# Block sums for a seven-product second layer: vector additions, or scalar copies with accumulating transfers

## The chip, the core and the metric

The kernel runs on one core of one Trainium2 chip. A core has a matrix engine (PE, with its weight loads PEld), a vector engine (DVE), a scalar engine (ACT), GpSimd (POOL) and a sync engine (SP); each takes its own instructions in order, and engines wait for each other and for transfers through semaphores. ACT, SP and POOL also issue DMAs, and the instruction that issues one stands in line with the engine's other work. The metric is the device time of one execution in microseconds (us), lower is better. Two runs of the kernel before took 622.52 and 622.56 us, a median of 622.54.

## The reference

A gated linear recurrence in float32, followed by a two-layer network with a leaky gate:

```
B, H, S, D = 4, 8, 768, 48
f = 1 / (1 + exp(-f_logit))
for t in range(S):
    state = f[:, :, t, :, None] * state + k[:, :, t] outer v[:, :, t]
    y[:, :, t] = q[:, :, t] @ state
x = y.transpose(0, 2, 1, 3).reshape(3072, 384)
h = x @ w_in                                   # 384 x 2048
g = maximum(h, 0) + alpha * minimum(h, 0)
out = g @ w_out                                # 2048 x 384
```

## The kernel before

The tokens are cut into twelve steps. A step is a pair of batches and a chunk of C = 128 positions: T = 256 tokens, in two halves `u` (one batch each). Every step goes through four generators: `prepare` (key P: loads, sigmoid, products of decays, on DVE and ACT), `carry` (O: the state), `attend` (S: the attention matrix `A`, the result `py` and its transposed copy `xT`) and `network` (n: both layers). A string written out by hand (`FIRST`, `USUAL`, lines 31 to 37) says in which order the pieces between two `yield`s are issued. PE, DVE and ACT keep exactly this order. While pass m of the network runs, `attend` of step m+1 and `prepare` of step m+2 are woven into it: "USUAL" is `S n2 S n2 O2 n Q n3 Q n Q S3 n Q S n Q n Q n`, where Q is a piece of the next `prepare`. POOL and SP are not in the manual order; a scheduler places what they issue.

The first layer runs in eight pieces `f` (L613). Each makes two blocks of 128 hidden rows in one PSUM bank `ph` (L618, twelve matmuls as the program writes them, shown in the trace as passes of 128x256), ACT writes `neg` = relu(-h) (L623, two buffers), and DVE writes the two blocks of `gate` (L625). Pass 0 multiplies `gate` by `w_out` plainly. Passes 1 to 11 split `gate` into token halves u and hidden halves j, split `w_out` into four blocks, and use seven products instead of eight (L657, 8 matmuls of the program, 16 in the trace, 2.60 us each product). For this they need four sums of gate blocks, S (one tile, one buffer), made by `sums` (L693) after f = 3 for the first four f and after f = 7 for the rest, and fixed differences of `w_out` blocks, made once (`halves_of_w_out`, L704). With a11 = (u0, j0), a12 = (u0, j1), a21 = (u1, j0), a22 = (u1, j1):

```
s1 = a21 + a22    s2 = s1 - a11    s3 = a11 - a21    s4 = a12 - s2
```

The five pieces behind f = 7 issue, on PE: `pa`, `pb`; then, after the pieces of `attend` between them (ACT copies `ad` into `A`, L563; PE multiplies `py`, L574), `pc`, `pd`; then `pa` and `pc` once more, added in place; then `pe`. DVE adds the products up (`plus`, L661; `kept`, `u2`, `u3` in `late["C"]`, called Csum in the profile). Four PSUM banks (`psn`) serve `ph` and all products, so a new one waits until the one before it in its bank has been read.

Between the pieces on ACT stand the copies of `qd` into `us` for the next step (L314), `kept` (L668), the eight copies into `A` (L563), the copies of `py` into `y` (L583) and the DMAs `xT<-y` (L603, dealt to SP, ACT and POOL). POOL issues the loads of q, f, k (L266) and v (L276). SP issues 16 small DMAs a step, `ksn<-kt` (L427), and the stores.

Of the kernel before, what the change touches and what calls it, by code (L numbers as in the profile page):

```python
# [8 lines left out]
F32 = mybir.dt.float32  # L9
# [5 lines left out]
AF = mybir.ActivationFunctionType  # L15
ALU = mybir.AluOpType

C = 128
# [3 lines left out]
U = 2  # L22
# [6 lines left out]
UP = 2.0 ** 16  # L29
# [29 lines left out]
def kernel(  # L59
# [30 lines left out]
    nc = tc.nc  # L90
    B, NC, _, HP, _ = qT.shape
    DM = v.shape[-1]
# [5 lines left out]
    T = U * C  # L98
# [16 lines left out]
    const = ctx.enter_context(tc.tile_pool(name="const", bufs=1))  # L115
# [9 lines left out]
    def bank(name):  # L125
        return psn.tile([128, 512], F32, tag="net", name=name)

    om = const.tile([128, NF], F32, tag="om", name="om")
    w_in_sb = const.tile([128, NK, DF], F32, tag="w_in", name="w_in_sb")
    w_out_sb = const.tile([128, NF, DM], F32, tag="w_out", name="w_out_sb")  # L130
    NH, DH = NF // 2, DM // 2
    gate = const.tile([128, NH, 2, T], F32, tag="gate", name="gate")
    lvl = const.tile([128, 2, DB], F32, tag="lvl", name="lvl")
    nc.scalar.dma_start(out=lvl, in_=masks)
    nc.scalar.dma_start(out=om, in_=alpha)
# [27 lines left out]
    for m in range(1, NB):  # L163
        lo = UO[m] + (4 if m == 1 else 0)
        n = NB - m
# [4 lines left out]
    for half in range(2):  # L170
        for m in range(1, NQ):
            n = NQ - m
# [436 lines left out]
    def network(bp, c, x):  # L609
        i = f"{bp}_{c}"  # L610
        xT = x["T"]
        plain = (bp, c) == steps[0]
        for f in range(NH):  # L613
            ph = bank(f"ph{f}_{i}")
            tiles = (2 * f, 2 * f + 1) if plain else (f, f + NH)
            for kt in range(NK):
                for j, m in enumerate(tiles):
                    nc.tensor.matmul(ph[:, j * T:(j + 1) * T], lhsT=w_in_sb[:, kt, m * 128:(m + 1) * 128],  # L618
                                     rhs=xT[:, kt], start=(kt == 0 and j == 0), stop=(kt == NK - 1 and j == 1),
                                     skip_group_check=True)  # L620
            neg = work.tile([128, 2, T], F32, tag="neg", name=f"neg{f}_{i}")
            phv = ph.rearrange("p (j t) -> p j t", j=2)
            nc.scalar.activation(neg, phv, AF.Relu, scale=-1.0)  # L623
            for j, m in enumerate(tiles):
                nc.vector.scalar_tensor_tensor(gate[:, m % NH, m // NH], neg[:, j], om[:, m:m + 1], phv[:, j],  # L625
                                               ALU.mult, ALU.add)
            if not plain and f % 4 == 3:
                sums(slice(f - 3, f + 1))
            yield

        def store(u, o):
            t0 = ((U * bp + u) * NC + c) * C
            nc.sync.dma_start(out=out[t0:t0 + C], in_=o)

        if plain:
            po = [bank(f"po{u}_{i}") for u in range(U)]
            for n, (f, u) in enumerate([(f, u) for f in range(NF) for u in range(U)]):
                nc.tensor.matmul(po[u][:, 0:DM], lhsT=gate[:, f % NH, f // NH, u * C:(u + 1) * C], rhs=w_out_sb[:, f],  # L638
                                 start=(f == 0), stop=(f == NF - 1))
                if n % 8 == 7 and n != U * NF - 1:  # L640
                    yield
            for u in range(U):
                o = work.tile([128, DM], F32, tag="o", name=f"o{u}_{i}")
                nc.scalar.activation(o, po[u][:, 0:DM], AF.Copy, scale=UP)
                store(u, o)
            yield
            return

        a11, a12, a22 = (lambda f, j=j, u=u: gate[:, f, j, u * C:(u + 1) * C] for j, u in ((0, 0), (1, 0), (1, 1)))
        s1, s2, s3, s4 = (lambda f, n=n: late["S"][:, n, f] for n in range(4))  # L650
        b11, t1, b21, b22 = (lambda f, r=r, d=d: w_out_sb[:, NH * r + f, DH * d:DH * (d + 1)]
                             for r, d in ((0, 0), (0, 1), (1, 0), (1, 1)))
        t2, t3, t4 = (lambda f, t=t: late[t][:, f] for t in ("t2", "t3", "t4"))

        def product(to, of, by, more=False):
            for f in range(NH):
                nc.tensor.matmul(to[:, 0:DH], lhsT=of(f), rhs=by(f), start=(f == 0 and not more), stop=(f == NH - 1),  # L657
                                 skip_group_check=True)

        def plus(to, of, by, scale=UP):  # L660
            nc.vector.scalar_tensor_tensor(to, of[:, 0:DH], scale, by, ALU.mult, ALU.add)  # L661

        o0, o1 = (work.tile([128, DM], F32, tag="o", name=f"o{u}_{i}") for u in range(U))
        kept, u2, u3 = (late["C"][:, n] for n in range(3))
        pa, pb = (bank(f"p{n}_{i}") for n in "ab")
        product(pa, a11, b11)
        product(pb, a22, t4)
        nc.scalar.activation(kept, pa[:, 0:DH], AF.Copy, scale=UP)  # L668
        yield
        pc, pd = (bank(f"p{n}_{i}") for n in "cd")  # L670
        product(pc, s2, t2)
        product(pd, s1, t1)
        plus(u2, pc, kept)
        yield
        product(pa, a12, b21, more=True)
        product(pc, s3, t3, more=True)
        plus(o0[:, DH:DM], pd, u2)
        nc.scalar.activation(o0[:, 0:DH], pa[:, 0:DH], AF.Copy, scale=UP)  # L678
        yield
        pe = bank(f"pe_{i}")  # L680
        product(pe, s4, b22)
        plus(u3, pc, kept)
        plus(o1[:, 0:DH], pb, u3, -UP)
        plus(o1[:, DH:DM], pd, u3)
        store(1, o1)
        yield
        plus(o0[:, DH:DM], pe, o0[:, DH:DM])
        store(0, o0)
        yield
# [3 lines left out]
    def sums(fs_):  # L693

        s = late["S"]
        u0, u1 = slice(0, C), slice(C, T)
        of = lambda j, u: gate[:, fs_, j, u]
        for to, x_, y_, op in ((s[:, 0, fs_], of(0, u1), of(1, u1), ALU.add),
                               (s[:, 1, fs_], s[:, 0, fs_], of(0, u0), ALU.subtract),
                               (s[:, 2, fs_], of(0, u0), of(0, u1), ALU.subtract),  # L700
                               (s[:, 3, fs_], of(1, u0), s[:, 1, fs_], ALU.subtract)):
            nc.vector.tensor_tensor(to, x_, y_, op)  # L702

    def halves_of_w_out():  # L704

        staging.close()
        pool = ctx.enter_context(tc.tile_pool(name="late", bufs=1))
        late["kt"] = pool
        late["S"] = pool.tile([128, 4, NH, C], F32, tag="S", name="S")
        late["C"] = pool.tile([128, 3, DH], F32, tag="C", name="Csum")  # L710
        for n in ("t2", "t3", "t4"):
            late[n] = pool.tile([128, NH, DH], F32, tag=n, name=n)
        yield
        b11, b12, b21, b22 = (w_out_sb[:, NH * r:NH * (r + 1), DH * d:DH * (d + 1)] for r in range(2) for d in range(2))
        t2, t3, t4 = (late[n] for n in ("t2", "t3", "t4"))

        for to, x_, y_, op in ((t3, b22, b12, ALU.subtract), (t2, t3, b11, ALU.add), (t4, t2, b21, ALU.subtract),
                               (b12, b12, b11, ALU.subtract)):
            for h in range(2):
                p = slice(h * NH // 2, (h + 1) * NH // 2)  # L720
                nc.vector.tensor_tensor(to[:, p], x_[:, p], y_[:, p], op)
            yield

    idle = bank("idle")
# [5 lines left out]
              for key, part in zip(keys, parts)}  # L730

    pieces["W"] = halves_of_w_out()

    with tc.manual_schedule(engines={mybir.EngineType.PE, mybir.EngineType.DVE, mybir.EngineType.Activation}):
        for _ in range(IDLE):
            nc.tensor.matmul(idle[0:32, 0:8], lhsT=ones[:, 0:32], rhs=ones[:, 0:8], start=True, stop=True)
        run = {}
        for n, step in enumerate(steps):
            x = {}
            for key, stage_ in zip("POSn", (prepare, carry, attend, network)):  # L740
                run[key, n] = stage_(*step, x)
        for key in order:
            next(run[key] if key in run else pieces[key[0]])
# [55 lines left out]
```

## Time and profile before

| what | value |
| --- | --- |
| median of two runs | 622.54 us |
| span of the profiled execution | 622.1 us |
| PE busy, PEld busy | 592.1 us (95%), 529.8 us (85%) |
| DVE busy | 497.1 us (80%) |
| ACT busy | 246.6 us (40%) |
| POOL busy | 63.0 us (10%) |
| PE in four passes from 225.38 us on | 47.59 us busy of 47.68 us each |
| `sums` on DVE, L702 | 88 instructions, 60.6 us busy in all, 688 ns one |

The span runs from the first to the last instruction of the execution that was profiled; no other time of that execution is given, and it lies 0.4 us below the median of the runs. Busy times of one engine overlap where instructions are pipelined, so a group of four copies takes less than four times one copy's duration; where the text needs a pace, it takes it from a row of the timeline that merges a group. `<-` in a row stands between output and input; x8 is a count; in brackets stand the idle time before a group and what ended it.

### The profile page before, as it was taken

The page shows a single profiled execution, that of the slowest core. Times are in us where ns is not written, and L with a number is a line of the kernel's source. Part 1 is how long each engine was busy: PE and PEld are TensorE (multiplying, and loading weights), DVE is VectorE, ACT ScalarE, POOL GpSimd, SP SyncE. Part 2 cuts the span into 40 slices and gives each one's busy share as a digit, 9 for nine tenths or more (in the row PEclk, how much of TensorE's full clock was granted, in tenths as well). Part 3 has the DMA queues.
Part 4 walks back from the last instruction along what each step waited for, and adds up shares of the span by engine and source line. Part 5 has one row for each costly group of instructions (what it writes and reads, how often), then busy time and mean ns, then how long its engine had stood idle before and what let it go on. Part 6 is the DMA issues. An engine that isn't in the chain of part 4 may idle for free.

```text
span 622.1 us, 19062 instructions
## 1 busy us (share of the span) xinstructions
PE 592.1 (95%) x8212; PEld 529.8 (85%) x8212; DVE 497.1 (80%) x997; ACT 246.6 (40%) x466; POOL 63.0 (10%) x117
## 2 busy tenths in 40 slices
PE   3568999999999999999999999999999999999997
PEld 3457866898899899899899899899889889889997
DVE  7588998899898798798798798798888888762261
ACT  5677862441641272262261351352253243223110
POOL 9120010001000011001001001001001000000000
PEclk9999999999999999999999999999999999999999
DMA  9964632014404314214313313413313401201000
GB/s 290 367 234 155 190 85 52 36 36 108 98 8 96 72 35 107 67 35 95 79 35 90 84 35 88 86 36 86 87 36 85 87 3 26 53 2 27 26 0 26
DMA packets 68116, 50.43 MB, mean 81 GB/s; under 512 B 47168, under 2 KB 60608, under 8 KB 68032
## 3 DMA queue, kind: packets, MB, share of 16 engines
q1 hardware_dynamic: 56656, 25.01, 15.6%
q0 software_dynamic: 6864, 22.35, 12.7%
q10 hardware_dynamic: 4512, 1.85, 1.7%
q8 instruction: 65, 1.06, 0.7%
q14 instruction: 19, 0.16, 0.1%
HBM read 36.21 MB, written 4.72 MB: 66 GB/s over the span
## 4 chain that ended last, share of the span: by engine, by line
PE 88%; DVE 6%; ACT 3%; issue 2%; DMA 1%; ACTq 0%; DVEq 0%
PE ph L618 39%; PE pc L657 9%; PE pa L657 8%; PE pd L657 5%; PE pe L657 4%; PE pb L657 4%; PE py L574 4%; PE po L638 3%; PE raw L520 3%; PE qu L535 3%; PE pd L484 3%; PE off L444 1%; PE xt L592 1%; DVE gate L625 1%; DMA f<-in_fT 1%
## 5 line engine op out<-in xcount | busy, mean ns | idle before, releaser
L618 PE MATMUL ph<-xT,w_in_sb 128*128 128x256 f32 x1152 | 258.7, 382 | 0.7 <-DVE Csum L661 0.7
L618 PEld LDWEIGHTS ph<-xT,w_in_sb 128*128 128x128 f32 x1152 | 216.4, 190 | 33.4 <-issue 2.3
L623 ACT ACTIVATE neg<-ph 128x512 f32<-128x512 f32 x96 | 57.4, 598 | 200.8 <-PE ph L618 139.5
L625 DVE SCALAR_TENSOR_TENSOR gate<-neg,om,ph 128x256 f32<-128x256 f32 x192 | 82.7, 478 | 50.6 <-ACT neg L623 50.4
L657 PE MATMUL pc<-t,S 128*128 128x192 f32 x352 | 61.7, 329 | 0.0
L657 PE MATMUL pa<-w_out_sb,gate 128*128 128x192 f32 x352 | 61.3, 327 | 0.1
L657 PEld LDWEIGHTS pa<-w_out_sb,gate 128*128 128x128 f32 x352 | 57.9, 190 | 1.0 <-DVE gate L625 0.4
L657 PEld LDWEIGHTS pc<-t,S 128*128 128x128 f32 x352 | 57.3, 190 | 0.6
L526 DVE COPY_PREDICATED ad<-mraw,raw 128x256 f32<-128x256 int32 (+1 forms) x96 | 42.4, 442 | 11.1 <-PE raw L520 8.6
L541 DVE COPY_PREDICATED ad<-mquad,qu 128x224 f32<-128x224 int32 (+6 forms) x140 | 42.0, 300 | 6.2
L419 ACT COPY A<-q 48x512 f32<-48x512 f32 x44 | 27.2, 619 | 36.1 <-DVE q L368 35.7
L563 ACT COPY A<-ad 32x256 f32<-32x256 f32 x96 | 38.7, 403 | 1.4
L330 DVE TENSOR_TENSOR us<-us,fs 128x768 f32<-128x768 f32 (+5 forms) x60 | 36.8, 614 | 0.0
L678 ACT ACTIVATE o<-pa 128x192 f32<-128x192 f32 x11 | 3.7, 332 | 75.2 <-PE pa L657 72.3
L661 DVE SCALAR_TENSOR_TENSOR Csum<-pc,Csum 128x192 f32<-128x192 f32 x22 | 7.9, 357 | 30.3 <-PE pc L657 30.1
L287 DVE TENSOR_TENSOR qd<-qd,f 128x768 f32<-128x768 f32 (+2 forms) x36 | 27.2, 756 | 6.0 <-ACT qd L282 6.0
L520 PEld LDWEIGHTS raw<-qd,k 48*32 48x32 f32 x1536 | 18.5, 109 | 15.3 <-issue 13.1
L520 PE MATMUL raw<-qd,k 48*32 48x80 f32 x1536 | 24.0, 243 | 7.6 <-issue 4.4
L702 DVE TENSOR_TENSOR S<-gate 128x512 f32<-128x512 f32 x44 | 30.3, 688 | 0.8
L657 PE MATMUL pe<-w_out_sb,S 128*128 128x192 f32 x176 | 30.4, 326 | 0.0
L657 PE MATMUL pd<-w_out_sb,S 128*128 128x192 f32 x176 | 30.4, 326 | 0.0
L657 PE MATMUL pb<-t,gate 128*128 128x192 f32 x176 | 30.4, 326 | 0.0
(101 smaller groups left out, 758.3 us busy)
## 6 DMA issues: line engine op xcount, KB each, us to landing
w_out_raw<-in_w_out SPq DMA_DIRECT2D x8, 767.8 KB, 5.8
w_in_raw<-in_w_in SPq DMA_DIRECT2D x8, 767.2 KB, 11.9
q<-in_qT POOLq DMA_DIRECT2D x11, 512.0 KB, 4.2
f<-in_fT POOLq DMA_DIRECT2D x11, 512.0 KB, 4.5
k<-in_kT POOLq DMA_DIRECT2D x11, 512.0 KB, 4.9
out<-o SPq DMA_DIRECT2D x24, 192.0 KB, 2.7
vs<-in_v POOLq DMA_DIRECT2D x22, 192.0 KB, 4.6
ksn<-kt SPq DMA_DIRECT2D x80, 32.0 KB, 2.0
```

Of the source, the lines that this page charges most:

```text
L287: nc.vector.tensor_tensor(qdv[d], qdv[d - 1][:, :, :, 1:5 - d], f[:, :, 1:5 - d].rearrange("p (g i) r -> p g i r", i=NB), ALU.mult)
L330: nc.vector.tensor_tensor(us[:, :, UO[m]:UO[m] + 4 * n].rearrange("p g (i r) -> p g i r", r=4), us[:, :, skip:skip + 4 * n].rearrange("p g ...
L419: nc.scalar.copy(A[halves(cc)[1], :, par * HP:(par + 1) * HP, CH * cc:CH * (cc + 1)], q3[rows(par)].rearrange("p (u h c) s t -> p u h c (s ...
L520: nc.tensor.matmul(raw[DB * j:DB * (j + 1), par, hp * C:hp * C + QW], lhsT=k[r_, g * DB:(g + 1) * DB], rhs=qd[r_, g], start=True, stop=True)
L526: nc.vector.copy_predicated(adu[:, :, :, d:4], mraw[:, d, :, d:4].bitcast(I32).unsqueeze(1).broadcast_to((128, H, NB, n)), rv[:, :, QO[d]: ...
L541: nc.vector.copy_predicated(ad[:, u, :, :, 4 * m:DB], mquad[:, lo:lo + n].bitcast(I32).unsqueeze(1).unsqueeze(1).broadcast_to((128, 2, HP, ...
L563: nc.scalar.copy(A[s_, u, :, s_], ad[s_, u].rearrange("p r h t -> p (r h) t"))
L618: nc.tensor.matmul(ph[:, j * T:(j + 1) * T], lhsT=w_in_sb[:, kt, m * 128:(m + 1) * 128], rhs=xT[:, kt], start=(kt == 0 and j == 0), stop=( ...
L623: nc.scalar.activation(neg, phv, AF.Relu, scale=-1.0)
L625: nc.vector.scalar_tensor_tensor(gate[:, m % NH, m // NH], neg[:, j], om[:, m:m + 1], phv[:, j], ALU.mult, ALU.add)
L657: nc.tensor.matmul(to[:, 0:DH], lhsT=of(f), rhs=by(f), start=(f == 0 and not more), stop=(f == NH - 1), skip_group_check=True)
L702: nc.vector.tensor_tensor(to, x_, y_, op)
```

## The change

The four sums are no longer made by DVE. ACT copies gate blocks into S, two of them negated, and four DMAs with an addition at the destination, issued by POOL, complete them; so S holds -s1, -s2, s3, s4, and the differences of `w_out` that go with the negated ones change their sign (the same number of DVE instructions, two of the four in another form). The gate tile is laid out by token half, so that a block of four f is one run of memory for each partition. `s3 t3` gets a bank of its own (`pf`) instead of being added onto `pc`. The order of the products becomes: `pa`, `pb`, (`py`), `pa` again, `pd`, `pf`, `pc`, `pe`; `u2` is issued one piece later, and `u3` is made from `u2`.

```diff
-    gate = const.tile([128, NH, 2, T], F32, tag="gate", name="gate")
+    gate = const.tile([128, 2, U, NH, C], F32, tag="gate", name="gate")
...
-                nc.vector.scalar_tensor_tensor(gate[:, m % NH, m // NH], neg[:, j], om[:, m:m + 1], phv[:, j],
+                nc.vector.scalar_tensor_tensor(gate[:, m // NH, :, m % NH], neg[:, j].rearrange("p (u t) -> p u t", u=U),
+                                               om[:, m:m + 1], phv[:, j].rearrange("p (u t) -> p u t", u=U),
                                                ALU.mult, ALU.add)
...
         product(pb, a22, t4)
         nc.scalar.activation(kept, pa[:, 0:DH], AF.Copy, scale=UP)
         yield
-        pc, pd = (bank(f"p{n}_{i}") for n in "cd")
+        pd = bank(f"pd_{i}")
+        product(pa, a12, b21, more=True)
+        product(pd, s1, t1)
+        nc.scalar.activation(o0[:, 0:DH], pa[:, 0:DH], AF.Copy, scale=UP)
+        yield
+        pf, pc = (bank(f"p{n}_{i}") for n in "fc")
+        product(pf, s3, t3)
         product(pc, s2, t2)
-        product(pd, s1, t1)
         plus(u2, pc, kept)
         yield
-        product(pa, a12, b21, more=True)
-        product(pc, s3, t3, more=True)
+        plus(u3, pf, u2)
         plus(o0[:, DH:DM], pd, u2)
-        nc.scalar.activation(o0[:, 0:DH], pa[:, 0:DH], AF.Copy, scale=UP)
-        yield
         pe = bank(f"pe_{i}")
         product(pe, s4, b22)
-        plus(u3, pc, kept)
...
-        for to, x_, y_, op in ((s[:, 0, fs_], of(0, u1), of(1, u1), ALU.add),
-                               (s[:, 1, fs_], s[:, 0, fs_], of(0, u0), ALU.subtract),
-                               (s[:, 2, fs_], of(0, u0), of(0, u1), ALU.subtract),
-                               (s[:, 3, fs_], of(1, u0), s[:, 1, fs_], ALU.subtract)):
-            nc.vector.tensor_tensor(to, x_, y_, op)
+        a = lambda j, u: gate[:, j, u, fs_]
+        n1, n2, s3, s4 = (s[:, n, fs_] for n in range(4))
+        nc.scalar.activation(s3, a(0, 1), AF.Copy, scale=-1.0)
+        nc.scalar.activation(n1, a(1, 1), AF.Copy, scale=-1.0)
+        nc.scalar.copy(n2, a(0, 0))
+        nc.scalar.copy(s4, a(1, 0))
+        for to, of in ((n1, s3), (s3, a(0, 0)), (n2, n1), (s4, n2)):
+            nc.gpsimd.dma_start(out=to, in_=of, accum_op=ALU.add)
...
-        for to, x_, y_, op in ((t3, b22, b12, ALU.subtract), (t2, t3, b11, ALU.add), (t4, t2, b21, ALU.subtract),
-                               (b12, b12, b11, ALU.subtract)):
+        for to, x_, y_, by in ((t3, b22, b12, None), (t2, t3, b11, -1.0), (t4, t2, b21, -1.0), (b12, b11, b12, None)):
...
```

More of the change, by code (lines that the diff above doesn't have):

```diff
@@ L637, in network @@
             for n, (f, u) in enumerate([(f, u) for f in range(NF) for u in range(U)]):
-                nc.tensor.matmul(po[u][:, 0:DM], lhsT=gate[:, f % NH, f // NH, u * C:(u + 1) * C], rhs=w_out_sb[:, f],
+                nc.tensor.matmul(po[u][:, 0:DM], lhsT=gate[:, f // NH, u, f % NH], rhs=w_out_sb[:, f],
                                  start=(f == 0), stop=(f == NF - 1))
@@ L647, in network @@
             return
-        a11, a12, a22 = (lambda f, j=j, u=u: gate[:, f, j, u * C:(u + 1) * C] for j, u in ((0, 0), (1, 0), (1, 1)))
+        a11, a12, a22 = (lambda f, j=j, u=u: gate[:, j, u, f] for j, u in ((0, 0), (1, 0), (1, 1)))
         s1, s2, s3, s4 = (lambda f, n=n: late["S"][:, n, f] for n in range(4))
@@ L695, in sums @@
         s = late["S"]
-        u0, u1 = slice(0, C), slice(C, T)
-        of = lambda j, u: gate[:, fs_, j, u]
-        for to, x_, y_, op in ((s[:, 0, fs_], of(0, u1), of(1, u1), ALU.add),
-                               (s[:, 1, fs_], s[:, 0, fs_], of(0, u0), ALU.subtract),
-                               (s[:, 2, fs_], of(0, u0), of(0, u1), ALU.subtract),
-                               (s[:, 3, fs_], of(1, u0), s[:, 1, fs_], ALU.subtract)):
-            nc.vector.tensor_tensor(to, x_, y_, op)
+        a = lambda j, u: gate[:, j, u, fs_]
[6 more added lines that the diff above has]
+            nc.gpsimd.dma_start(out=to, in_=of, accum_op=ALU.add)
     def halves_of_w_out():
@@ L715, in halves_of_w_out @@
         t2, t3, t4 = (late[n] for n in ("t2", "t3", "t4"))
-        for to, x_, y_, op in ((t3, b22, b12, ALU.subtract), (t2, t3, b11, ALU.add), (t4, t2, b21, ALU.subtract),
-                               (b12, b12, b11, ALU.subtract)):
+        for to, x_, y_, by in ((t3, b22, b12, None), (t2, t3, b11, -1.0), (t4, t2, b21, -1.0), (b12, b11, b12, None)):
             for h in range(2):
                 p = slice(h * NH // 2, (h + 1) * NH // 2)
-                nc.vector.tensor_tensor(to[:, p], x_[:, p], y_[:, p], op)
+                if by is None:
+                    nc.vector.tensor_tensor(to[:, p], x_[:, p], y_[:, p], ALU.subtract)
+                else:
+                    nc.vector.scalar_tensor_tensor(to[:, p], x_[:, p], by, y_[:, p], ALU.mult, ALU.subtract)
             yield
```

## The prediction

> **What bounds the kernel now.** I read the page's busy shares and chain first, then the chain in order of time over one pass, then the timelines of ACT, PE and DVE around the sums.
>
> ```profile
> span 622.1 us, 19062 instructions
> PE 592.1 (95%) x8212; PEld 529.8 (85%) x8212; DVE 497.1 (80%) x997; ACT 246.6 (40%) x466; POOL 63.0 (10%) x117
> ...
> PE 88%; DVE 6%; ACT 3%; issue 2%; DMA 1%; ACTq 0%; DVEq 0%
> ```
>
> PE carries 88% of the chain. In time order, pass 5 (and passes 3 to 9 alike, 47.7 us apart) is PE alone:
>
> ```profile
> 357.91 10.56 PE ph L618 x48
> 368.46 2.60 PE pa L657 x16
> 371.06 2.60 PE pb L657 x16
> 373.66 2.09 PE py L574 x64
> 375.76 2.80 PE pc L657 x16
> 378.55 2.60 PE pd L657 x16
> 381.15 2.60 PE pa L657 x16
> 383.75 2.60 PE pc L657 x16
> 386.35 2.60 PE pe L657 x16
> 388.95 0.78 PE raw L520 x56
> ```
>
> No gap is left, and the change keeps PE's matmuls: seven products of 2.60 us before and after. So from about 150 us on it can only add waits for PE. What matters is how much room the neighbours have. ACT, ahead of `py`:
>
> ```profile
> 368.55 0.60 ACT L623 ACTIVATE neg<-ph 128x512 f32<-128x512 f32 x1 [2.04 <-DVE gate L625]
> 369.04 2.17 ACT L314 COPY us<-qd 128x256 f32<-128x256 f32 x4
> 371.10 0.33 ACT L668 ACTIVATE Csum<-pa 128x192 f32<-128x192 f32 x1
> 371.33 3.34 ACT L563 COPY A<-ad 32x256 f32<-32x256 f32 x8
> 375.80 1.08 ACT L583 COPY y<-py 128x512 f32<-128x512 f32 x2 [1.13 <-PE py L574]
> ```
>
> The eighth copy into `A` ends at 371.33 + 3.34 = 374.67. `py` (64 matmuls in 2.09 us, 0.033 each) needs it from its 37th matmul on (in pass 2 it stopped there, after 36, until that copy was done, 0.06 before): 373.66 + 36 x 0.033 = 374.85. ACT is idle 60% of the time, yet at this place it has 0.1 us of slack.
>
> **Part 1: the four copies after f = 7, passes 3 to 9.** In the built order they stand on ACT between `neg` of f = 7 and L314; behind them wait L314, `kept`, the eight copies into `A`, and so `py`. The first needs the first gate block of f = 7. DVE starts that pair at 369.18 and one takes 0.48 (L625, mean 478 ns): 369.66, and 0.05 for the semaphore. One copy of 128x512: the nearest rows are `y<-py`, two in 1.08, and `neg`, 598 ns alone; bounds 0.40 (L563, 32x256) and 0.63 (L419, four of 48x512 in 2.52). I take 0.54, the same size: 4 x 0.54 = 2.16. L314 starts at 369.71 + 2.16 = 371.87 instead of 369.04, 2.83 later, and everything behind shifts with it. Less the slack, PE waits **2.7 us** in `py` (bounds 2.2 to 3.1). Nothing gives it back: the chain ph, neg, gate, copies, L314, A, py starts from PE itself in each pass. DVE's freed 4 x 0.6 us behind f = 7 does not help, since DVE's next piece waits for `us` from L314, which now ends at 374.04 (before, DVE took it at 373.94).
>
> **Part 2: `u2` and `u3`.** In the built program `pe` lies in the bank that `pc` leaves, and the next `ph` in the bank of `pf`. DVE:
>
> ```profile
> 378.67 0.36 DVE L661 SCALAR_TENSOR_TENSOR Csum<-pc,Csum 128x192 f32<-128x192 f32 x1 [1.52 <-PE pc L657]
> ...
> 385.04 0.41 DVE L330 TENSOR_TENSOR us<-us,fs 128x256 f32<-128x256 f32 x1
> ...
> 389.50 0.36 DVE L661 SCALAR_TENSOR_TENSOR Csum<-pc,Csum 128x192 f32<-128x192 f32 x1
> ```
>
> `pc` ended at 378.49 and `u2` began 0.18 later, for 0.36. A bank's way back to PE shows in pass 1's row:
>
> ```profile
> 152.34 8.04 PE L618 MATMUL ph<-xT,w_in_sb 128*128 128x256 f32 x36 [0.74 <-DVE Csum L661]
> ```
>
> DVE's Csum there ran from 151.93 for 0.35, so 0.06 more. `pe` waits 0.18 + 0.36 + 0.06 = **0.6 us** (DVE is by then idle, waiting for `pc`). Behind `u2` on DVE stands a piece of `prepare` from 385.04 to 389.50, 4.46 us, then `u3`, which frees the bank of the next `ph`. From the start of `u2`: DVE 0.27 + 4.46 + 0.36 + 0.06 = 5.15; PE 0.42 + `pe` 2.60 + `raw` and `qu` 1.72 (388.95 to 390.67) = 4.74. `ph` waits **0.4 us** (bounds 0 and 0.8).
>
> Behind that piece on DVE are `kt`, so the 16 DMAs `ksn<-kt` on SP: they start 1.6 us later against PE, `pd` (L484) 1.0 later. SP's last issue ended at 400.96, landing takes 2.0, need at 403.95: 1.0 of room becomes 0.4. I cost it at 0; without the cover 0.5 a pass. `o<-pa` (L678) now stands ahead of `y<-py` and waits for `pa`, so `y` and the `xT` DMAs go 2.9 later: last ACT issue 379.0 + 4.8 landing = 383.8 becomes 386.7, against need at 390.6, which itself moves by 1. Cost 0.
>
> Passes 3 to 9: 7 x (2.7 + 0.6 + 0.4) = 25.9.
>
> **Part 3: the other passes.** Pass 10 has no L314 and `kept` waited for `pa` until 561.89; the copies end at 562.66 (371.87 + 190.79, the distance of the two passes' `pa`): 0.8 + 0.6 = 1.4. Pass 2: `A`'s second half started at 182.23; with the copies from 178.5 it starts at 183.0: 0.8 + 0.6 + 0.4 = 1.8. Pass 1 is bound by DVE and ACT: the first four copies hold up `neg` of f = 4 and the sigmoid chain (3.6 us on ACT), DVE's gates come 2.1 later although its sums (120.60 to 123.14) are gone, and the second `pa`, now right after `pb`, waits for `kept` behind copies and L314, 3.1; with 0.2 at the end 5.4 (bounds 0 to 7). Pass 11: 0.6. The copies after f = 3 otherwise end before `neg` of f = 4 is due (359.1 + 1.27 for `A<-off` = 360.4, due 360.78). `w_out` differences and gates keep count and size: 0.
>
> **Part 4: the accumulating DMAs.** Eight a pass on POOL, 256 KB each. First adds wait for copies, the second and third for the first, the fourth for the third. No row shows an accumulate. Bounds from issue to landing: 2.0 (fastest `xT<-y`) and 10.7 (slowest v load). These rows are nearest:
>
> ```profile
> q<-in_qT POOLq DMA_DIRECT2D x11, 512.0 KB, 4.2
> f<-in_fT POOLq DMA_DIRECT2D x11, 512.0 KB, 4.5
> k<-in_kT POOLq DMA_DIRECT2D x11, 512.0 KB, 4.9
> vs<-in_v POOLq DMA_DIRECT2D x22, 192.0 KB, 4.6
> ```
>
> A load moves 512 KB twice (read, write), an accumulate 256 KB three times; I take X = 4.6. First four: the gates of f = 3 begin at 356.26, so two copies are done and POOL starts at 358.0; fourth issued at 358.7 + 2X; then the q load in its queue (0.73), so the second four start at 370.9 (copies) or 360.1 + 2X. The second four serve the second half of each product. `py` ends at 378.5 with its wait; `pa` 2.8, `pd` 2.6 and half of `pf` make 385.2; the other half of `pf`, `pc`, the 0.6 and half of `pe` 391.0. They land at 370.9 + 2X = 380.1 and, at the latest of copies and queue, 371.6 + 3X = 385.4; a v load ahead of the last waits for `py` (378.5) and adds nothing. Hidden, cost 0. From X = 6.0 on the queue decides (360.8 + 5X against 391.0), 5 us a pass for each us more. xT's two DMAs on POOL come after (y at 382.6).
>
> [...]
>
> **Sum.** 25.9 + 1.4 + 1.8 + 5.4 + 0.6 = 35.1 on the span of 622.1: 657.2. The runs' median lies 0.4 above the span: **658 us**, +5.7%.
>
> **Rivals.**
> - *Accumulates late* (X over 6). For it: a strictly serial chain, semaphores between, slow landings up to 8.3 among these loads. Against: medians 4.2 to 4.9 at twice the size. At X = 7: 360.8 + 35 = 395.8, 4.8 us late in ten passes: 658 + 48 = 706; at X = 8 756.
> - *Not slower:* the copies are covered. If the copies into `A` did not shift by more than 0.3 us a pass, `py` would keep its place. Left are 1.0 in passes 2 to 9 and 0.6 in 1, 10 and 11: 9.8, so 632 us, within 2%. For it: ACT idles 60%. Against: the slack above, in every pass; ACT's idle lies elsewhere. Four copies in 0.3 us is below any row.
> - *Faster through DVE:* 60.6 us of additions leave an engine that is 80% busy. DVE binds only before 150 us, where two blocks of sums stand (120.60 and 131.82, 2.6 each): 617 us with all else free.
> - That the change does not do what it says is excluded by the built order: 88 copies, 88 accumulates, 88 additions gone.
>
> **How the numbers follow.** Forecast as worked (648 to 668): 0.70; accumulates late: 0.20; covered: 0.06; faster: 0.02; the rest 0.02, between 636 and 648. The range 645 to 705 holds the first, the milder half of the second and some of the rest, 0.8. Two per cent, 610 to 635, is about what this kernel's measurement tells from no change: faster 0.02, same 0.06, slower 0.92.
>
> **What would show it.** Right: PE idle 2.7 us in all before `py`'s later matmuls, released by ACT L563, and 0.6 before `pe`, released by DVE Csum; a period of 51.4 instead of 47.7; DVE idle some 6 us before `u2`. Wrong: PE idle before `pd`, `pf` or `pe` released by a DMA on S (accumulates over 6 us), `pd` L484 released by `ksn`, or ACT's copies at another pace than 0.54.

## The result, and the profile after

Two runs of the changed kernel took 653.15 and 654.17 us, a median of 653.66 against 622.54: a ratio of 1.049 (95% interval 1.046 to 1.053), slower. (In the ratios below, the one run that took over 1.5% more than the fastest of its kernel, 695.48 us of the kernel with the old order, is left out.) The page of the profile after, its span, busy shares and chain:

```profile
span 651.4 us, 19306 instructions
PE 596.5 (92%) x8212; PEld 528.2 (81%) x8212; DVE 440.2 (68%) x909; ACT 290.6 (45%) x554; POOL 141.2 (22%) x205
...
PE 61%; ACT 15%; DVE 13%; DMA 4%; issue 4%; SPq 1%; ACTq 1%; DVEq 0%
```

DVE lost 57 us of work, ACT and POOL took on 122, and PE's matmuls stayed what they were. The chain, which was PE alone to 88%, now goes through ACT and DVE for more than a quarter of the span. What PE waited for, from the list of waits (us in total, times, longest):

```profile
PE py L574 <- ACT A L563: 17.0, 24, 1.2
...
PE pe L658 <- DVE Csum L662: 7.0, 11, 1.5
...
PE pa L658 <- ACT Csum L669: 2.8, 1, 2.8
```

Before, the other two were absent, and the first was:

```profile
PE py L574 <- ACT A L563: 0.3, 1, 0.3
```

No wait for a DMA on S stands in the list after. Pass 5 on PE (start, us, operation; in brackets the idle time before it and what ended it):

```profile
330.98 2.76 PE L658 MATMUL pa<-w_out_sb,gate 128*128 128x192 f32 x16
333.58 2.76 PE L658 MATMUL pb<-t,gate 128*128 128x192 f32 x16
337.50 0.34 PE L574 MATMUL py<-A,vs 128*64 128x64 f32 x4 [1.16 <-ACT A L563]
338.34 1.18 PE L574 MATMUL py<-A,vs 128*64 128x64 f32 x32 [0.50 <-ACT A L563]
340.02 1.03 PE L574 MATMUL py<-A,vs 128*64 128x64 f32 x28 [0.50 <-ACT A L563]
340.99 2.87 PE L658 MATMUL pa<-w_out_sb,gate 128*128 128x192 f32 x16
...
348.89 2.76 PE L658 MATMUL pc<-t,S 128*128 128x192 f32 x16
352.18 2.87 PE L658 MATMUL pe<-w_out_sb,S 128*128 128x192 f32 x16 [0.53 <-DVE Csum L662]
```

`py` now stops three times for A, each time for the next of ACT's copies. Why A is late shows on ACT, here in pass 6 (the rows that the prediction calls pass 5 are pass 6 by this count, whose pass 1 starts at 102.47 before; the passes are alike, and nothing in its sum changes):

```profile
382.40 0.60 ACT L623 ACTIVATE neg<-ph 128x512 f32<-128x512 f32 x1 [2.04 <-PE ph L618]
383.54 0.63 ACT L700 ACTIVATE S<-gate 128x512 f32<-128x512 f32 x1 [0.55 <-DVE gate L625]
...
385.11 0.61 ACT L703 COPY S<-gate 128x512 f32<-128x512 f32 x1
385.63 2.12 ACT L314 COPY us<-qd 128x256 f32<-128x256 f32 x4
387.56 0.35 ACT L669 ACTIVATE Csum<-pa 128x192 f32<-128x192 f32 x1
387.81 3.32 ACT L563 COPY A<-ad 32x256 f32<-32x256 f32 x8
```

The four copies run from 383.54 to 385.63, 0.52 each. L314 begins 3.23 after the start of `neg` where it was 0.49 after it (368.55 to 369.04 before), so everything behind it is 2.74 later. Back in pass 5, `u2`, for which `pe` waits, and `u3`; between them stands a piece of `prepare`:

```profile
351.77 0.36 DVE L662 SCALAR_TENSOR_TENSOR Csum<-pc,Csum 128x192 f32<-128x192 f32 x1 [6.17 <-PE pc L658]
...
356.48 0.36 DVE L662 SCALAR_TENSOR_TENSOR Csum<-pf,Csum 128x192 f32<-128x192 f32 x1
```

DVE, which was to be relieved, stands idle 6.17 us there, waiting for PE. The accumulating transfers, from the list of DMAs (KB each, median us from issue to landing), with two loads that share their queue:

```profile
S<-S POOLq DMA_DIRECT2D x66, 256.0 KB, 3.9
q<-in_qT POOLq DMA_DIRECT2D x11, 512.0 KB, 5.3
f<-in_fT POOLq DMA_DIRECT2D x11, 512.0 KB, 6.4
...
S<-gate POOLq DMA_DIRECT2D x22, 256.0 KB, 3.4
```

Where the time went, measured from the first `ph` of one pass to that of the next:

| stretch | before | after | change | forecast |
| --- | --- | --- | --- | --- |
| up to pass 1's first `ph` | 102.47 | 99.00 | -3.5 | 0 |
| pass 1 | 49.87 | 54.43 | +4.6 | +5.4 |
| pass 2 | 47.63 | 50.01 | +2.4 | +1.8 |
| passes 3 to 9, mean of one | 47.68 | 51.08 | +3.4 | +3.7 |
| pass 10 | 45.98 | 47.22 | +1.2 | +1.4 |
| pass 11, to the end of the span | 42.37 | 43.17 | +0.8 | +0.6 |

The first row can't be put down to the change: the traces of the eight other kernels below gave 99.0 to 103.8 there, with no order by what was changed. Of the 3.5 us, 2.0 are PE gaps that the profile books to "issue", and 1.5 are PE's own busy time, 77.7 against 76.2 for the same matmuls. Passes 1 to 11 lost 32.8 us.

### The profile page after: what moved, and what is told of

The parts are those of the page before. It is cut to its first block, busy times and chain, and to the rows that moved or that the text cites. A ratio compares the mean times of both kernels' runs of the same rounds, so it can differ in the third digit from the quotient of the medians.

```text
span 651.4 us, 19306 instructions
## 1 busy us (share of the span) xinstructions
PE 596.5 (92%) x8212; PEld 528.2 (81%) x8212; DVE 440.2 (68%) x909; ACT 290.6 (45%) x554; POOL 141.2 (22%) x205
## 4 chain that ended last, share of the span: by engine, by line
PE 61%; ACT 15%; DVE 13%; DMA 4%; issue 4%; SPq 1%; ACTq 1%; DVEq 0%
PE ph L618 33%; PE pa L658 5%; ACT A L563 4%; PE po L639 3%; ACT us L314 3%; PE pd L658 3%; PE pe L658 3%; PE pc L658 2%; PE pf L658 2%; DMA xT<-y 2%; PE pd L484 2%; PE py L574 2%; PE qu L535 2%; PE raw L520 2%; DVE gate L625 2%
## 5 line engine op out<-in xcount | busy, mean ns | idle before, releaser
L705 POOL DMA_DIRECT2D S<-S x66 | 64.9, 988 | 205.1 <-ACT S L701 126.9
L658 PE MATMUL pa<-w_out_sb,gate 128*128 128x192 f32 x352 | 62.7, 330 | 3.3 <-ACT Csum L669 2.8
L662 DVE SCALAR_TENSOR_TENSOR Csum<-pc,Csum 128x192 f32<-128x192 f32 x11 | 3.9, 358 | 76.6 <-PE pc L658 76.5
L266 POOL DMA_DIRECT2D k<-in_kT x11 | 8.0, 731 | 184.4 <-PE raw L520 184.4
L574 PE MATMUL py<-A,vs 128*64 128x64 f32 x768 | 30.8, 234 | 17.7 <-ACT A L563 17.0
L574 PEld LDWEIGHTS py<-A,vs 128*64 128x64 f32 x768 | 26.6, 144 | 23.6 <-ACT A L563 21.4
L658 PEld LDWEIGHTS pe<-w_out_sb,S 128*128 128x128 f32 x176 | 28.3, 190 | 10.2 <-DVE Csum L662 10.2
L705 POOL DMA_DIRECT2D S<-gate x22 | 18.9, 859 | 73.3 <-issue 27.1
L658 PE MATMUL pf<-t,S 128*128 128x192 f32 x176 | 30.5, 327 | 0.0
L658 PE MATMUL pc<-t,S 128*128 128x192 f32 x176 | 30.4, 326 | 0.0
```

The source lines that it names most:

```text
L574: nc.tensor.matmul(py[64 * par:64 * par + 64, u, o:o + CH], lhsT=vs[bp][:, cc, u, hd * D:hd * D + 64], rhs=A[:, u, par * HP + hp, CH * cc: ...
L705: nc.gpsimd.dma_start(out=to, in_=of, accum_op=ALU.add)
```

## The experiments

Each kernel is compared with runs of the kernel before beside it (medians of 621.37 and 621.64 us); ratios are against those, with a 95% interval. The ratio of the changed kernel, 1.049, is against its own two runs of before (622.54), so differences between ratios carry some 0.2% of that.

### Layout and sign alone

The additions stay on DVE, with the signs of the change; the order of the products is the old one.

```diff
-    gate = const.tile([128, NH, 2, T], F32, tag="gate", name="gate")
+    gate = const.tile([128, 2, U, NH, C], F32, tag="gate", name="gate")
...
+        nc.vector.scalar_tensor_tensor(n1, a(0, 1), -1.0, a(1, 1), ALU.mult, ALU.subtract)
+        nc.vector.tensor_tensor(n2, a(0, 0), n1, ALU.add)
+        nc.vector.tensor_tensor(s3, a(0, 0), a(0, 1), ALU.subtract)
+        nc.vector.tensor_tensor(s4, a(1, 0), n2, ALU.add)
```

> The kernel before with two of the change's edits alone: gate laid out by token half, and the sums (still VectorE additions, at their old places) in the negated form, with the old order of the products. My theory: neither the layout nor the form costs anything, since the row of the gate blocks keeps its 0.48 us each (0.478 before, 0.477 after) and the products' matmuls keep 0.33; the time stays at that of the kernel before, 621 to 622.5, period 47.7. Rival: part of what the run with the new order and VectorE sums lost (13.7 us by the medians) is the layout's and not the order's; then this kernel is 3 us or more slower, 624 to 635.

Measured: 621.97 us, ratio 0.9997 (0.9977 to 1.0016). Pass 1 takes 49.88 us and passes 3 to 9 47.71 each, against 49.87 and 47.68 in the kernel before. Layout and sign cost nothing that can be measured, and what follows belongs to the other two parts of the change.

### The new order alone

The changed kernel with the additions back on DVE.

```diff
-        nc.scalar.activation(s3, a(0, 1), AF.Copy, scale=-1.0)
-        nc.scalar.activation(n1, a(1, 1), AF.Copy, scale=-1.0)
-        nc.scalar.copy(n2, a(0, 0))
-        nc.scalar.copy(s4, a(1, 0))
-        for to, of in ((n1, s3), (s3, a(0, 0)), (n2, n1), (s4, n2)):
-            nc.gpsimd.dma_start(out=to, in_=of, accum_op=ALU.add)
+        nc.vector.scalar_tensor_tensor(n1, a(0, 1), -1.0, a(1, 1), ALU.mult, ALU.subtract)
+        nc.vector.tensor_tensor(n2, a(0, 0), n1, ALU.add)
+        nc.vector.tensor_tensor(s3, a(0, 0), a(0, 1), ALU.subtract)
+        nc.vector.tensor_tensor(s4, a(1, 0), n2, ALU.add)
```

> Only the second part of the change: the new order and banks of the products, all sums by the vector engine (negated form), no copies, no accumulates. Theory: pe waits for u2 by 0.6 to 0.7 us in each of 11 passes and ph by 0.3 in 9 of them: 622.5 + 10 = 632 to 633 us. Rival (all of the loss is in the copies): 622 to 624.

Measured: 635.05 us, ratio 1.022 (1.019 to 1.024), 2 us above the expectation. A pass of 3 to 9 takes 48.5 us, 0.8 more than before, with the wait of 0.53 in front of `pe`: this is Part 2 of the forecast, alone. The rest is mostly pass 1, which took 55.36 us against 49.87. There DVE is behind with its work: `u2` starts at 148.32 with DVE busy up to it, 3.6 us after `pc` has ended. PE's row in pass 1:

```profile
148.74 4.55 PE L658 MATMUL pe<-w_out_sb,S 128*128 128x192 f32 x16 [3.98 <-DVE Csum L662]
```

Not only the wait of 3.98 is new: `pe` itself took 4.55 in place of 2.8 (the last section returns to it).

### Copies and transfers for the first half only

The changed kernel, with the sums behind f = 7 on DVE.

```diff
+        if fs_.start:
+            nc.vector.scalar_tensor_tensor(n1, a(0, 1), -1.0, a(1, 1), ALU.mult, ALU.subtract)
...
+            return
         nc.scalar.activation(s3, a(0, 1), AF.Copy, scale=-1.0)
```

> The changed kernel with the sums behind f = 7 made by the vector engine (in the negated form), those behind f = 3 still by copies and accumulates. Theory (the four copies behind f = 7 stand ahead of the copies into A and hold py): py's wait of 2.6 us in passes 3 to 9 goes, so do the 2.8 before the second pa in pass 1, 1.3 in pass 2 and 0.5 in pass 10: 653.7 - 22.8 = 631 us, a period of 48.5 us; the waits before pe (0.5 by the row) and ph stay. Rival (the new order of the products with its late u2 costs most): the time stays above 645.

Measured: 637.04 us, ratio 1.026 (1.022 to 1.030). The wait in `py` is gone, and a pass of 3 to 9 takes 48.5 us, as with the new order alone. So the copies behind f = 3 and their accumulates are free in these passes, the copies behind f = 7 bring the wait of 2.6 us a pass, and between this kernel and the changed one lie 2.3 points of the ratio. Most of the 6 us above the expectation is pass 1: 55.83 us, 5.96 more than before, where the expectation comes to 51.6. There `pe` waited 3.99 for `u2` and then took 4.43, at a granted clock of 0.50 from 150.1 to 152, close to the 4.55 of the new order alone; pass 2 has 1.0 more than expected, also in front of `pe`. The step from the kernel with the new order alone (1.022 to 1.026) can't be told from none by these intervals.

### The copies moved behind those into A

The copies behind f = 7 are issued at the end of the piece that copies into A, so that nothing of A waits for them.

```diff
-            if not plain and f % 4 == 3:
-                sums(slice(f - 3, f + 1))
+            if not plain and f == 3:
+                sums(slice(0, 4))
...
+        sums(slice(4, NH))
```

> The changed kernel with the four copies behind f = 7 moved on the scalar engine behind the eight copies into A; the accumulates start some 4.7 us later against PE. Theory: py no longer waits (2.6 less), but the second accumulate of the late half now lands after the second half of pf is due, so PE waits there 1.4 to 1.6 us a pass for a DMA on S: net 1 us a pass less, 644 to 647 us, and the wait has moved from py to pf. Rival (place of the copies does not matter): 653. Rival (accumulates are far from the limit): 631.

Measured: 663.21 us, ratio 1.066 (1.063 to 1.069): slower than the changed kernel, and the expectation missed it. Pass 5 on PE:

```profile
341.31 2.15 PE L574 MATMUL py<-A,vs 128*64 128x64 f32 x64
343.39 2.87 PE L658 MATMUL pa<-w_out_sb,gate 128*128 128x192 f32 x16
346.09 1.46 PE L658 MATMUL pd<-w_out_sb,S 128*128 128x192 f32 x8
347.98 1.57 PE L658 MATMUL pd<-w_out_sb,S 128*128 128x192 f32 x8 [0.42 <-DMA S<-S]
349.38 1.46 PE L658 MATMUL pf<-t,S 128*128 128x192 f32 x8
352.41 1.57 PE L658 MATMUL pf<-t,S 128*128 128x192 f32 x8 [1.56 <-DMA S<-gate]
```

`py` runs through, 64 matmuls in 2.15. But the first copy starts 6.4 us after `pa` instead of 1.4, so all four accumulates are 5.0 later; and PE reaches `pd` and `pf` 2.6 earlier, since it no longer stands still in `py`. Together 7.6 us, and the transfers become the wait: passes 3 to 9 take 51.0 us on the mean, as in the changed kernel, and passes 1, 2, 10 and 11, in which the room was smaller, lose 0.9, 2.4, 1.7 and 1.4 on top of it. One wait took the place of the other.

### The old order with copies and transfers

```diff
-        pd = bank(f"pd_{i}")
-        product(pa, a12, b21, more=True)
+        pc, pd = (bank(f"p{n}_{i}") for n in "cd")
+        product(pc, s2, t2)
         product(pd, s1, t1)
...
+        product(pa, a12, b21, more=True)
+        product(pc, s3, t3, more=True)
```

> Only the first part: sums by copies and accumulates, products in the order of before (pc with s2 right behind py, s3 added into pc). Theory: the waits before pe and ph go (1.0 a pass), but s2 is the third accumulate and is now needed first: its late half lands 0.8 us after pc needs it in passes 3 to 9, some 3 us late in pass 1 and 5.7 in pass 11, which has no py in between: 655 to 662 us, PE waiting in pc for a DMA on S. Rival (the new order is only a cost): 643 to 645.

Measured: 687.88 us, ratio 1.102 (1.094 to 1.110), 26 us over the expectation. Two things were wrong with it. The first is the size of the wait for S: `pc` now needs its second half right behind `py`, three products (7.9 us) earlier than in the new order, and waited 25.1 us for it in seven passes, where the terms of the expectation add up to some 14. The second was not thought of. Pass 2 on PE, and the same stretch in windows (stretch, its length, PE busy, PEclk, DMA share, GB/s):

```profile
195.23 1.57 PE L658 MATMUL pc<-t,S 128*128 128x192 f32 x8
203.80 2.93 PE L658 MATMUL pc<-t,S 128*128 128x192 f32 x8 [7.00 <-DMA S<-S]
206.52 4.36 PE L658 MATMUL pd<-w_out_sb,S 128*128 128x192 f32 x16
```

```profile
197.00:199.00 2.00, 0.00 (x0) 1.00 1.06 169
199.00:201.00 2.00, 0.00 (x0) 0.63 1.19 127
201.00:203.00 2.00, 0.00 (x0) 0.50 0.87 253
...
207.00:209.00 2.00, 2.00 (x8) 0.50 0.60 152
209.00:211.00 2.00, 2.00 (x11) 0.81 0.00 0
```

PE stood still from 196.8, the granted clock fell to one half at about 200, and stayed there for some 6 us after the matmuls had begun again: 8 of them took 2.93 in place of 1.46, 16 took 4.36 in place of 2.76. In passes 1 to 11 PE's gaps add up to 42.5 us of 585.5, against 27.9 of 552.4 in the changed kernel, so PE was busy some 18.5 us longer: the same matmuls ran slower. With the 11 us of waiting that is more than the missing 26. The runs of this kernel differ among themselves in step with it: 679.67 us at a mean granted clock of 0.977, 686.26 at 0.968, 689.49 at 0.965, 695.48 at 0.953.

### The wait filled with other matmuls

The same kernel, with discarded matmuls in the wait of passes 1, 2, 10 and 11. It tells whether the products were slow because PE had stood still, or because transfers wrote to the same memory.

```diff
+        fill = {1: 24, 2: 24, 10: 12, 11: 24}.get(steps.index((bp, c)), 0)
+        for f in range(NH):
+            if f == NH // 2:
+                for n in range(fill):
+                    nc.tensor.matmul(pd[:, 0:DH], lhsT=a22(n % NH), rhs=t4(n % NH), start=(n == 0), stop=(n == fill - 1),
+                                     skip_group_check=True)
+            nc.tensor.matmul(pc[:, 0:DH], lhsT=s2(f), rhs=t2(f), start=(f == 0), stop=(f == NH - 1),
+                             skip_group_check=True)
-        product(pc, s2, t2)
```

> The kernel with the old order and the accumulating DMAs, in which TensorE waited 6.1, 7.0, 3.0 and 5.3 us for S in passes 1, 2, 10 and 11 and then ran the second half of pc and the whole of pd at about twice their usual time (2.93 for 8 matmuls in place of 1.46, 4.36 for 16 in place of 2.76) at a granted clock of 0.50. Here 24 matmuls (12 in pass 10) whose result is thrown away stand in that wait: the wait is filled, and nothing else is moved. Theory, the granted clock falls because TensorE stands idle for some 3 us or longer: with the wait filled the products behind it run at their usual time, 2.9 us saved in passes 1, 2 and 10 and 1.5 in pass 11, about 10 us: 676 to 680 against 688. Rival, the products are slow because the accumulating DMAs write the operand's memory at the same time: pc and pd stay at 2.9 and 4.4 behind the fillers, and the time stays at 680 to 695. The dips of the clock that began in other passes (3 and 7) stay in either case.

Measured: 683.64 us (682.16 to 683.96), ratio 1.098 (1.095 to 1.101). Pass 2 on PE:

```profile
194.90 7.96 PE L676 MATMUL pd<-t,gate 128*128 128x192 f32 x48
202.69 1.46 PE L678 MATMUL pc<-t,S 128*128 128x192 f32 x8
204.00 2.76 PE L658 MATMUL pd<-w_out_sb,S 128*128 128x192 f32 x16
```

Behind the fill `pc` and `pd` take their usual 1.46 and 2.76, in passes 1, 2, 10 and 11 alike; in pass 2 at a granted clock of 1.00 from 202 to 210, with the DMAs busy for 0.95 of their time from 202 to 206. So it was the standing still and not the transfers; the kernel with the new order alone says the same, since its `pe` took 4.55 us behind a wait of 3.98 although it has no accumulate at all. The slow `pc` in passes 3 and 7 stayed, as expected: 5.1 and 3.8 us for its 16 matmuls, against 2.76. The time does not decide it, for the intervals of the two kernels overlap. The gain of 10 us did not come, because the fill was mis-sized: a matmul of the program is two in the trace, 24 took 7.96 us, longer than the waits of 5.3 to 7.0. From the start of `pc` to the `pa` behind it, pass 2 gained 2.4 and pass 10 2.3, pass 11 lost 0.8; pass 1, up to `py`, gained 1.5.

### One and two links more in the chain of transfers

How far were the accumulates of the changed kernel from being late? Zeros are added into n1 ahead of the late half's four, once in the first kernel and twice in the second.

```diff
+        if fs_.start:
+            for _ in range(1):
+                nc.gpsimd.dma_start(out=n1, in_=late["Z"].broadcast_to((128, 4, C)), accum_op=ALU.add)
         for to, of in ((n1, s3), (s3, a(0, 0)), (n2, n1), (s4, n2)):
```

> The changed kernel with one accumulate more (of zeros, 256 KB into n1) ahead of the four of f = 4 to 7, so that each of these lands one link of the chain later; the program's result is unchanged. My theory: the chain of the late half has about 4.3 us to spare in a steady pass (its second accumulate has landed by 349.2 on the clock of the changed kernel's pass 6 and is wanted at 353.5), and one link is 4.2 to 4.4: the time grows only where the late half has no other work in front of it (pass 11, about 3.6), so 654 to 658. Rival, by which the accumulates are already on the path in steady passes: 4 us more in each of nine, 690. Rival, by which they are far from it: 653 to 655 in this run and no more than 661 with two links.

Measured: 672.63 us, ratio 1.082 (1.078 to 1.087), between both theories. Per pass it is clear: passes 3, 4, 6, 7 and 9 keep 51.0 to 51.2 us, so there the link was spare. In pass 5 it was not quite, as PE's rows show:

```profile
356.33 1.46 PE L658 MATMUL pf<-t,S 128*128 128x192 f32 x8
358.98 1.57 PE L658 MATMUL pf<-t,S 128*128 128x192 f32 x8 [1.19 <-DMA S<-gate]
```

Passes 5 and 8 grew by 2.8 and 1.5. The expectation failed outside the steady passes. Passes 2 and 10 grew by 3.5 and 3.9: PE waits only 1.3 and 0.5 us in `py` there, the accumulates have that much less room, and `pf` waited 1.74 and 2.00 for one. In pass 10 slow matmuls came on top, the second half of `pf` 2.35 and `pc` 3.71 in place of 1.46 and 2.76; in pass 2 the waits are 1.9 of the 3.5, and three products took 3.06 to 3.19 in place of some 2.8, which no run here explains. Pass 11 grew by 6.6, not 3.6, with `pf` at a granted clock of 0.50 (4.36 us) behind a wait of 3.4. Pass 1 grew by 1.8 without any wait for a DMA. Its wait for `kept` is that of the changed kernel, 2.83, but the `pa` behind it was slow:

```profile
139.43 4.55 PE L658 MATMUL pa<-w_out_sb,gate 128*128 128x192 f32 x16 [2.83 <-ACT Csum L669]
```

In the changed kernel this `pa` took 2.87.

> The same with two accumulates of zeros ahead: 8.4 to 8.8 us later, of which 4.3 are spare. My theory: a PE wait for S of about 4.3 us in each of the nine steady passes and about 8 in pass 11, 653.7 + 39 + 8 = 700, and more if the granted clock falls behind waits of that length (two half-clock products behind each would add up to 2.9 us a pass, 726). Rival, accumulates far from the path: 654 to 661.

Measured: 717.43 us, ratio 1.152 (1.148 to 1.156), in the range of the first theory. Every pass pays; 3 to 9 take 54.6 to 58.3 us. From the list of PE's waits:

```profile
PE pd L658 <- DMA S<-S: 30.1, 9, 7.3
...
PE pf L658 <- DMA S<-gate: 11.9, 6, 2.4
```

So the accumulates of the changed kernel were hidden in the steady passes with about one link, 4 us, to spare, and no more; 2.6 of that room were PE's own delay in `py`.

## Why the prediction was right

The forecast of 658 us lies 4 above the measured 653.7. Step by step:

- **Part 1** (2.7 us a pass, in `py`): right in cause and size. From the start of `pa` to the start of the product behind `py` a pass went from 7.39 to 10.01 us, +2.62; the copies' pace was 0.52 (0.54 forecast), L314 came 2.74 later (2.83). The kernel with the first half's copies alone loses this wait and, in passes 3 to 9, nothing else; with the copies moved behind those into A it is gone as well. Only its place differed: PE stops ahead of `py`'s first matmuls too, not from the 37th on.
- **Part 2** (0.6 in front of `pe`, 0.4 in front of `ph`): right in front of `pe`, where a product of 2.60 and the wait take 3.29 us from the start of `pc`, 0.69 more than the product; too much in front of `ph`, since from `pe` to `ph` passes 3 to 9 grew by 0.2 on the mean. The kernel with the new order alone shows both together as 0.8 a pass. With Part 1 that makes 3.5; the period grew by 3.4, the rest of the pass being 0.1 shorter.
- **Part 3**: the sum holds (9.2 forecast for passes 1, 2, 10 and 11, 9.0 measured), but in pass 1 (5.4 forecast, 4.6 measured) it is in part luck, for the terms are others. The second `pa` did wait 2.83 for `kept` behind the copies (3.1 forecast). But the last gates, forecast 2.1 later, came 0.6 later; a wait of 1.50 in front of `pe` for `u2` was not in the working; and the 0.74 in front of pass 2's first `ph` went away. The order alone, with the additions on DVE, loses 5.5 there, more than the whole change: `pe` waited 3.98 and 3.99 for `u2` in the two kernels with the late sums on DVE, so freeing DVE saved part of what the order cost.
- **Part 4** (accumulates hidden): right, by about one link. X was 3.4 to 3.9 at the median, not 4.6, and 3.2 to 6.0 over all of them. The rival of late accumulates (706 us) was nearer than its X of 7 said: one link more made it true in some passes, two in all. That an accumulate moves its 256 KB three times, the ground given for 4.6, no run shows.
- **The sum**: 32.8 us in passes 1 to 11 against 35.1; the steady passes' 0.3 us make most of the difference. The step from span to time was mis-sized: the runs lie 1.8 above their own spans, not 0.4, so the profiled execution of before was itself about 1.4 longer than its runs. Its start-up also took 3.5 more than that of the profiled execution after. These three, 2.3 and 3.5 less 1.4, make the 4 us by which the forecast was high; the middle one is chance.

The rival "not slower" falls with Part 1, the rival "faster through DVE" with the row of 6.17 us idle in front of `u2`. Among the parts, the new order costs 2.2%, the copies behind f = 7 2.3%; layout, signs and the first half's copies nothing that these runs can tell. No version here beats the kernel before, and these runs point at none: from pass 1 on its PE has two gaps over 0.15 us in all, 0.74 us in front of pass 2's first `ph` and 0.28 in pass 2's `py`.

## What to carry to other kernels

An engine that is idle 60% of the time can have no room at the one place where work is put: look at what stands behind that place in its queue and when that is needed, not at its share. Two hidden waits can cover each other: before taking one away, work out what the engine then reaches earlier, and whether the other chain is there in time. And before a transfer's latency is taken off an engine by a chain of dependent DMAs, count the links from the first issue to the last use.

## What the hardware showed that was not expected

TensorE's granted clock was 1.00 over the whole span of the profiled executions before and after. In other kernels it fell to 0.50: by the windows of the profile in passes 1, 2, 3, 6, 7, 10 and 11 of the old order with the transfers, in pass 1 with copies and transfers for the first half only, and in pass 11 with one link more. These stretches at one half lasted 3.4 us (three of them), 6.8 (five) and, in pass 2 of the old order, 10.2, as worked out from the means of the windows. The length of a wait alone does not tell whether the clock falls:

| kernel | wait of PE | granted clock behind it, in a window (us) | the next product |
| --- | --- | --- | --- |
| changed, pass 1 | 2.83 | 1.00 (133 to 139) | `pa`, 16 matmuls in 2.87 |
| one link more, pass 1 | 2.83 | no window there | `pa`, 16 in 4.55 |
| copies behind A, pass 1 | 3.29 | 1.00 (142 to 147) | `pd`, 8 in 1.57 |
| old order, pass 10 | 2.98 | 0.50 (623 to 629) | `pc`, 8 in 2.93 |
| old order, pass 7 | 1.17, 0.50, 0.50 | 0.50 (464 to 468) | `pc`, 16 in 5.14 |
| changed, pass 9 | 1.15, 0.50, 0.50 | 1.00 (542 to 548) | `pa`, 16 in 2.87 |

Behind 3.29 us the clock stayed, behind 2.98 it fell, and in the old order it also fell in passes 3, 6 and 7 at the three waits in `py`, none over 1.2 us, while the changed kernel, with the same three waits in each of seven passes, stayed at 1.00. What decides, these runs do not settle. After the matmuls had begun again behind a wait of 2 us or more, the half clock lasted 3.0 to 6.1 us in the six stretches that the windows show; the wait of 7.00 us thus cost close to 10: 7.00, and 1.47 and 1.60 in the products behind it.

A DMA that adds at its destination, 256 KB within SBUF, took 3.2 us from issue to landing at the least and 3.4 to 3.9 at the median. From one issue to that of the next which depends on it, the chain took 3.7 to 6.3 us at its first link (median 4.0) and 4.8 to 6.6 at its last (median 5.3), and POOL was busy for 0.85 to 1.2 us to issue one. Most of the loads beside it became slower at the median: those of f, 512 KB, went from 4.5 to 6.4 us, of q from 4.2 to 5.3, of v from 4.6 to 5.2, while those of k stayed (4.9 and 4.7).
